# A recurrence feeding a gated MLP on one core: the hand-written start order, with the fourth group ahead of weight block 2

## The chip, the cores and the metric

One core of a Trainium2 chip runs the kernel. The metric is device time in microseconds (us): the median over runs of the time of the core. The kernel before takes 528.25 us, the median of 3 runs (527.22 to 528.74).

## The reference

```python
# attention part: B, H, S, D = 4, 8, 768, 48; state is D x D for each of the 32 (batch, head) pairs
for t in range(S):
    kt, vt, rt = k[:, :, t], v[:, :, t], r[:, :, t]
    cur = einsum('bhd,bhe->bhde', u * kt, vt)
    y[:, :, t] = einsum('bhd,bhde->bhe', rt, state + cur)
    state = w * state + einsum('bhd,bhe->bhde', kt, vt)
# MLP part: 3072 tokens, d_model 384, d_ff 1536
x = y.transpose(0, 2, 1, 3).reshape(B * S, H * D)
out = (sigmoid(x @ w_gate) * (x @ w_val)) @ w_out
```

## The kernel before

**Tiling.** The 768 time steps are cut into 12 chunks of 64 and the heads into 2 halves; a chunk and a half make a *group*, 24 in all, numbered in the order of work: group 0 and 1 are the halves of chunk 0, group 2 and 3 those of chunk 1, and so on. In a group the recurrence becomes small matmuls: scores of keys with queries, scores with values, queries with the state, and the outer products of keys and values that update the state. Two chunks together (512 tokens) are one tile of the MLP; the first tile is also worked in two parts of 256 tokens, the part of chunk 0 (`a`) and that of chunk 1 (`b`), so that the MLP can begin before chunk 1 is done. The MLP's 1536 inner columns are 12 blocks of 128, and a block of weights (gate, value and output together) is loaded once, joined from its 8-byte words and split into a rounded high part and a low rest; three matmuls make each product (lines 518 and 526 to 535). Block `0` in the start stands for what line 239 keeps in buffer 11.

**The order.** Tile's own scheduling is switched off (line 89): each engine runs its instructions in the order in which the program issues them. The first 60 to 70 us are written by hand: `START` (lines 43 to 58) is a list of steps, and the loop of lines 682 to 689 issues them one after the other. The rest follows from the loop of lines 711 to 743. An engine sees only its own steps of the list, so a step's place matters against the other steps of its engine.

The steps that are spoken of below, with `n` a group and `f` a weight block:

- `L.n`, `X.n`, `W.f` (SyncE): load the group's channels (queries and keys, line 104), its tokens (keys and values, line 109), a block's weights (line 242). Channels and tokens have 3 buffers each (lines 75 and 76), so `X.3` waits until the last reader of group 0's tokens, its outer products, is done.
- `F.n` (SyncE): six small transfers that bring x of one head pair into place in the MLP's input (line 501).
- `A.n`, `R.n` or `Rv.n`, `k.n`: keys with bonus (ScalarE, line 296), scaled queries (GpSimd or VectorE, line 309), scaled keys (VectorE, line 320). `T.n`, `Tv.n`: token keys (GpSimd, VectorE, line 324).
- `Z.n`, `K.n` (TensorE line 392, VectorE line 400): scores, and their copy out of PSUM under a mask.
- `I.n` (TensorE, line 354): the outputs of a group, queries with the state and then, behind a drain, scores with values. They go to two PSUM banks, called the group's pair here.
- `O.n` (TensorE, line 354): the outer products; for a group that `outer` names in line 426 they go to two accumulator banks, for others into the rest of the group's pair.
- `h.n` (ScalarE, line 493) and `l.n` (VectorE, line 497): x's high and low part out of the pair. `d.n` (ScalarE, line 447) and `s.n` (VectorE, line 466) or `sa.n` (ScalarE, line 468): the state decayed, and the outer products added or copied to it.
- `c.f`, `j.f`, `w.f`, `o.f` or `ov.f`: a weight block's upper halves taken out (ScalarE, line 249), words joined (VectorE, line 256), high part rounded (ScalarE, line 264), low rest (GpSimd or VectorE, line 267).
- `u.f`, `v.f` (TensorE, line 531): gate and value products of a block; `g.f` sigmoid (ScalarE, line 544), `m.f` product (VectorE, line 548), `H.f` high part (ScalarE, line 553), `q.f` or `qv.f` low part (line 557), `D.f` the output product (TensorE, line 573). A trailing `a` or `b` is a half of the first tile.
- `N.k` (TensorE, line 641): k matmuls of 128x512 on the identity, whose result nobody reads.

**PSUM.** A gate product, a value product and each half of a pair take one bank from a ring of three, in turn:

```python
    ring = ctx.enter_context(tc.tile_pool(name="ring", bufs=3, space=PSUM))   # line 72
        return ring.tile([P, 512], F32, name="ring")                          # line 84, one_bank
        yb[n] = one_bank(), one_bank()                                        # line 360, outputs
            w, o, k = (whi[f], wlo[f]), one_bank(), 0                         # line 527, up_one
```

So each new taker waits for the readers of what was taken three turns earlier. A pair's readers are `h`, `l` and `s` of its group; a gate product's reader is `g`, a value product's is `m`.

Of the kernel before, what the change touches and what calls it, by code (L numbers as in the profile page):

```python
# [40 lines left out]


START = """
ta L.0 tov.0 tc tb W.0 ts.0 L.1 ts.1 X.0 tz W.1 tk L.2 X.1 to.1 ti.1 X.2 ti.0 A.0 R.0 W.2 k.0 c0.0
tp tr Z.0 tt A.1 K.0 c0.1 tn k.1 I.0 Rv.1 j0.1 h.0 l.0 Tv.0 Z.1 c.1 j0.0 O.0 A.2 j.1 w0.0 sa.0 N.5
T.2 K.1 F.0 w.1 W.3 Rv.2 I.1 T.1 N.4 k.2 L.3 o0v.0 h.1 L.4 Z.2 w0.1 W.4 O.1 X.3 l.1 o0.1 s.1 u.0a
g.0a K.2 v.0a o.1 m.0a c.2 I.2 O.2 R.3 d.2 j.2 u.1a A.3 N.3 H.0a g.1a k.3 h.2 q.0a s.2 v.1a w.2 l.2
m.1a Z.3 T.3 A.4 H.1a N.4 R.4 K.3 c.3 k.4 I.3 O.3 F.2 L.5 W.8 o.2 D.0a X.4 h.3 L.6 Z.4 W.5 l.3 d.3
W.6 L.7 s.3 X.5 u.0b X.6 g.0b j.3 v.0b c.4 w.3 u.2 j.4 qv.1a m.0b H.0b g.2 v.2 q.0b K.4 w.4 Rv.5
u.1b T.4 A.5 v.1b g.1b m.1b D.0b k.5 H.1b I.4 ov.3 O.4 m.2 A.6 R.6 q.1b Z.5 k.6 L.8 d.4 D.1a W.7 h.4  # L50
o.4 s.4 H.2 D.1b K.5 c.6 l.4 Tv.5 u.3 c.5 g.3 j.6 v.3 j.5 qv.2 I.5 h.5 Z.6 l.5 R.7 L.9 A.7 m.3 X.8
d.5 D.2 ub K.6 H.3 O.5 k.7 s.5 w.5 q.3 u.4 c.8 T.6 ov.5 c.7 g.4 v.4 j.7 w.6 m.4 u.5 ov.6 g.5 v.5 I.6
Y.8 R.8 Z.7 W.9 d.6 O.6 W.10 X.7 w.7 W.11 H.4 s.6 X.9 D.3 j.8 h.6 qv.4 w.8 l.6 D.4 m.5 H.5 F.6 ov.7
qv.5 u.6 c.9 g.6 K.7 v.6 ov.8 m.6 Tv.7 H.6 u.7 qv.6 g.7 k.8 v.7 j.9 m.7 w.9 D.5 o.9 u.8 g.8 H.7 v.8
q.7 c.10 D.6 j.10 m.8 I.7 H.8 Z.8 O.7 d.7 R.9 h.7 w.10 s.7 D.7 b.8 ov.10 u.9 l.7 qv.8 g.9 c.11 v.9
F.7 Y.9 j.11 m.9 D.8 w.11 ov.11 u.10 g.10 H.9 qv.9 v.10 m.10 H.10 u.11 qv.10 g.11 t.8 i.8 v.11 K.8
k.9 m.11 D.9 H.11 t.9 D.10 q.11 b.9 T.9 i.9 T.8
"""


# [869 lines left out]
```

## Time and profile before

| | us |
|---|---|
| median of 3 runs | 528.25 (527.22 to 528.74) |
| the profiled execution's own time | 528.38 |
| its span, first to last instruction | 526.6 |
| TensorE busy | 509.7 (97% of the span) |
| VectorE, ScalarE, GpSimd busy | 202.6, 186.1, 187.2 (35 to 38%) |

The span is 1.78 us shorter than the execution's time. Busy shares are means over the whole span; the first 60 us differ from the rest, and that is where the change lies. In the rows of the timeline a row is a run of like instructions: its start in us from the start of the span, its length in us, engine, line, operation, and how many; a note in brackets is idle time of the engine ahead of it and what ended it. Matmul ends are modelled, so lengths between rows are taken from start to start.

### The profile page before, as it was taken

To read this page: it belongs to the slowest core of one execution; us is meant where nothing else is said; L and a number is where in the kernel's file an instruction comes from. 1 tells how busy PE (TensorE), PEld (TensorE's weight loads), DVE (VectorE), ACT (ScalarE), POOL (GpSimd) and SP (SyncE) were. 2 spreads that over 40 slices of the span, in tenths; PEclk is the share of its full clock that TensorE was granted. 3 is DMA by queue.
4 is the path that set the end of the run, shared out by engine and by line. 5 is a ranking of instruction groups with operands and counts; after the bars stand their busy time and mean duration, and the time that the engine had idled before them with its cause. 6 is when DMAs were issued, how large, how long until landed. Compare 5 with 4: busy or idle time off the path is not lost.

```text
span 526.6 us, 11976 instructions
## 1 busy us (share of the span) xinstructions
PE 509.7 (97%) x5220; PEld 421.4 (80%) x5220; DVE 202.6 (38%) x345; ACT 186.1 (35%) x395; POOL 187.2 (36%) x158
## 2 busy tenths in 40 slices
PE   3899999999999999999999999999999999999995
PEld 3689788888888788888888888888888888888884
DVE  7877865545242243242341432431442211111112
ACT  5587864534223134233133332331431221311211
POOL 4454402214545252453452452552352111111120
PEclk9899999999999999999999999999999999999999
DMA  8949654123213030420230420312400000100001
GB/s 318 368 144 421 262 191 167 34 75 96 76 64 88 10 107 4 145 88 19 78 98 12 148 87 1 97 36 72 147 17 2 11 7 14 61 0 1 0 2 65
DMA packets 15579, 47.84 MB, mean 91 GB/s; under 512 B 2368, under 2 KB 4928, under 8 KB 14112
## 3 DMA queue, kind: packets, MB, share of 16 engines
q1 hardware_dynamic: 15376, 46.74, 25.5%
q8 instruction: 43, 0.70, 0.6%
q10 hardware_dynamic: 144, 0.26, 0.1%
q14 instruction: 16, 0.13, 0.1%
HBM read 39.92 MB, written 4.72 MB: 85 GB/s over the span
## 4 chain that ended last, share of the span: by engine, by line
PE 95%; DVE 2%; DMA 1%; issue 1%; ACT 0%; SPq 0%; DVEq 0%; ACTq 0%
PE ring L531 56%; PE acc L573 29%; PE ring L354 7%; PE sc L392 3%; DMA chan<-in_ch 1%; DVE score L400 1%; DVE wf L256 0%; PE acc L641 0%; DVE chan L320 0%; ACT dec L296 0%; DVE sg L586 0%; DVE dec L309 0%; DVE xt L497 0%; DVE toks L324 0%; PE acc L354 0%
## 5 line engine op out<-in xcount | busy, mean ns | idle before, releaser
L531 PE MATMUL ring<-xt,wx 128*128 128x512 f32 (+1 forms) x1332 | 306.5, 384 | 0.0
L531 PEld LDWEIGHTS ring<-xt,wx 128*128 128x128 f32 x1332 | 245.2, 188 | 49.8 <-ACT sg L544 0.3
L557 POOL TENSOR_TENSOR h<-sg,h 128x512 fp32r<-128x512 f32 (+1 forms) x65 | 87.1, 1340 | 252.4 <-ACT h L553 252.4
L573 PE MATMUL acc<-h,wx 128*128 128x512 f32 (+1 forms) x666 | 161.3, 387 | 0.0
L573 PEld LDWEIGHTS acc<-h,wx 128*128 128x128 f32 x666 | 121.2, 188 | 25.0 <-DVE h L557 0.2
L548 DVE TENSOR_TENSOR sg<-ring,sg 128x512 f32<-128x512 f32 (+1 forms) x74 | 50.0, 676 | 235.0 <-PE ring L531 233.5
L544 ACT ACTIVATE sg<-ring 128x512 f32<-128x512 f32 (+1 forms) x74 | 43.2, 584 | 156.3 <-PE ring L531 156.3
L553 ACT CAST h<-sg 128x512 fp32r<-128x512 f32 (+1 forms) x74 | 45.0, 609 | 144.1 <-DVE sg L548 137.8
L309 POOL TENSOR_TENSOR dec<-chan,tabk 128x512 f32<-128x512 f32 x21 | 27.7, 1319 | 14.3 <-PE ring L354 14.0
L497 DVE TENSOR_TENSOR xt<-ring,xt 112x256 fp32r<-112x256 f32 (+1 forms) x52 | 19.9, 418 | 32.6 <-ACT xt L493 32.6
L324 POOL TENSOR_TENSOR toks<-toks,tabn 128x384 f32<-128x384 f32 x19 | 23.7, 1253 | 12.5 <-ACT wx L264 9.5
L330 POOL TENSOR_TENSOR dec<-dec,toks 128x384 f32<-128x384 f32 x16 | 16.3, 1017 | 26.9 <-DMA dec<-in_rt 26.7
L320 DVE TENSOR_TENSOR chan<-chan,tabk 128x512 f32<-128x512 f32 x24 | 24.8, 1034 | 0.6 <-ACT dec L296 0.6
L392 PE MATMUL sc<-dec,chan 48*64 48x64 f32 x768 | 17.2, 231 | 7.7 <-DVE chan L320 7.6
L400 DVE COPY_PREDICATED score<-masks,sc 128x512 f32<-128x512 int32 x32 | 23.9, 748 | 1.9 <-PE sc L392 1.1
L447 ACT ACTIVATE state<-state,pw 112x96 f32<-112x96 f32 x80 | 23.4, 362 | 1.8 <-PE ring L354 1.8
L392 PEld LDWEIGHTS sc<-dec,chan 48*64 48x64 f32 x768 | 14.8, 145 | 8.9 <-POOL dec L309 7.6
L466 DVE TENSOR_TENSOR state<-state,ring 48x192 f32<-48x192 f32 (+1 forms) x52 | 17.9, 350 | 8.1 <-PE ring L354 4.3
L256 DVE SCALAR_TENSOR_TENSOR wf<-wr,top 128x1152 int32<-128x1152 int32 (+1 forms) x13 | 16.8, 1304 | 9.5 <-ACT top L249 6.0
L354 PE MATMUL ring<-score,toks 64*48 64x64 f32 (+1 forms) x768 | 16.6, 223 | 3.7 <-issue 2.3
L493 ACT CAST xt<-ring 112x256 fp32r<-112x256 f32 (+1 forms) x52 | 16.7, 363 | 6.6 <-PE ring L354 6.4
L267 POOL TENSOR_TENSOR wx<-wf,wx 128x1152 fp32r<-128x1152 f32 (+1 forms) x5 | 12.5, 2507 | 18.3 <-ACT wx L264 18.3
(63 smaller groups left out, 254.7 us busy)
## 6 DMA issues: line engine op xcount, KB each, us to landing
wr<-in_wt SPq DMA_DIRECT2D x11, 1152.0 KB, 9.1
...
```

The costliest lines, as they stand in the source:

```text
L309: eng.tensor_tensor(v4(t[:, 0]), v4(chan[n][:, 0]), bc2(table_of(n)[:, :, ::-1]), ALU.mult)
L320: eng.tensor_tensor(v4(k), v4(k), bc2(table_of(n)), ALU.mult)
L324: eng.tensor_tensor(v4(k), v4(k), bc2(tabn[:, 4 * g : 4 * g + 4]), ALU.mult)
L354: nc.tensor.matmul(to[bank][64 * half : 64 * half + m, cs], lhsT, rhs, start=first, stop=stop, skip_group_check=True,)
L392: nc.tensor.matmul(sc[64 * gm : 64 * gm + 64, be, o : o + C], kk[row, cs : cs + C], rr[row, cs : cs + C], start=True, stop=True,)
L400: nc.vector.copy_predicated(t.rearrange("q (b m i) -> q b m i", b=2, m=4), masks[:, m].bitcast(I32).unsqueeze(1).unsqueeze(1).broadcast_to ...
L531: nc.tensor.matmul(o[:, self.cols], w[a][:, g * DM + kt * P : g * DM + (kt + 1) * P], self.x[:, kt, b, self.cols], start=(k == 0), stop=(k ...
L544: nc.scalar.activation(sg[:, c], self.pair[f][0][:, c], AF.Sigmoid, scale=UP)
L548: nc.vector.tensor_tensor(sg[:, c], self.pair.pop(f)[1][:, c], sg[:, c], ALU.mult)
L553: nc.scalar.copy(out=h[:, 0, c], in_=sg[:, c])
L557: eng.tensor_tensor(h[:, 1, c], self.sg.pop(f)[:, c], h[:, 0, c], ALU.subtract)
L573: nc.tensor.matmul(self.acc[d][:, self.cols], w[a][:, 2 * DM + d * P : 2 * DM + (d + 1) * P], h[:, b, self.cols], start=(f == 0 and k == 0 ...
```

## The change

In `START` the 188 steps between two unchanged ends become 185 in a new order. Group 3 comes earlier: `L.3` and `X.3` stand ahead of `W.2`, and `Z.3`, `K.3`, `I.3` and the work before them ahead of the preparing of block 2 (`j.2`, `w.2`) and of its products (`u.2`, `v.2`), which now come behind both halves of block 1. In chunk 0, group 0's outer products `O.0` go behind `I.1`, into accumulator banks, and their copy into the state (`sa.0`) goes behind group 1's copy of x (`h.1`). `W.3` and `W.4` are loaded behind `F.2`. Block 2's low rest moves from GpSimd to VectorE (`o.2` to `ov.2`), group 5's queries from VectorE to GpSimd (`Rv.5` to `R.5`). Of the 16 matmuls of `N` (`N.5`, `N.4`, `N.3`, `N.4`) one step of 7 is left. Nothing that is read later is left out.

```diff
-tp tr Z.0 tt A.1 K.0 c0.1 tn k.1 I.0 Rv.1 j0.1 h.0 l.0 Tv.0 Z.1 c.1 j0.0 O.0 A.2 j.1 w0.0 sa.0 N.5
-T.2 K.1 F.0 w.1 W.3 Rv.2 I.1 T.1 N.4 k.2 L.3 o0v.0 h.1 L.4 Z.2 w0.1 W.4 O.1 X.3 l.1 o0.1 s.1 u.0a
...
+Z.0 L.3 tt A.1 K.0 c0.1 tn k.1 I.0 Rv.1 j0.1 h.0 l.0 Tv.0 Z.1 c.1 j0.0 A.2 j.1 w0.0 T.1 N.7 w.1 T.2
+F.0 K.1 Rv.2 I.1 O.0 k.2 o0v.0 X.3 Z.2 L.4 R.3 h.1 W.2 w0.1 L.5 sa.0 l.1 O.1 o0.1 A.3 s.1 u.0a g.0a
...
     def outer(n):
         k, v = toks[n][:, 0], toks[n][:, 1]
-        if n in (1,):
+        if n in (0, 1):
             ob[n] = [pacc.tile([P, 512], F32, name=f"acc{i}") for i in (1, 2)]
```

**TensorE, between the first half of block 1's gate product and the outputs of group 3** (`u.1a` to `I.3`). Before, from the last idle matmul of `N.3` (`acc_540`) to the first of `N.4` (`acc_610`):

```order
L641 MATMUL acc_540<-spare 128x512
L531 MATMUL ring<-xt,wx 128x256 x9
L392 MATMUL sc<-dec,chan 64x64 x16
L392 MATMUL sc<-chan,dec 64x64 x16
L641 LDWEIGHTS spare
L641 MATMUL acc_610<-spare 128x512
```

and now, from `u.1a` to the first matmuls of `I.3`:

```order
L531 MATMUL ring<-xt,wx 128x256 x9
L392 MATMUL sc<-dec,chan 64x64 x16
L392 MATMUL sc<-chan,dec 64x64 x16
L531 MATMUL ring<-xt,wx 128x256 x9
L354 MATMUL ring<-dec,state 64x64 x2
```

The seven idle matmuls of this place are gone, and group 3's scores stand ahead of the value product `v.1a` instead of behind it.

**ScalarE, around the sigmoid of block 1's first half.** Line 249 with `wr_173` (before) and `wr_404` (now) takes out the upper halves of block 2's weights; the sigmoid of block 1's first half, `g.1a`, is the second row of line 544 of each order. Before:

```order
L544 ACTIVATE sg_450<-ring_440 128x256
L249 ACTIVATE top0_120<-wr_173 128x1152
L447 ACTIVATE state_99<-state_99,pw_101 112x96 x4
L296 ACTIVATE dec_518<-chan_365,wu_93 128x128 x4
L553 CAST h_544<-sg_450 128x256
L544 ACTIVATE sg_546<-ring_526 128x256
```

and now:

```order
L544 ACTIVATE sg_453<-ring_443 128x256
L447 ACTIVATE state_99<-state_99,pw_101 112x96 x4
L493 CAST xt_252<-ring_470 112x2x128
L493 CAST xt_252<-ring_471 112x2x128
L553 CAST h_537<-sg_453 128x256
L249 ACTIVATE top0_120<-wr_404 128x1152
L544 ACTIVATE sg_578<-ring_527 128x256
```

Now `g.1a` stands right behind line 249 instead of four rows after it, and the weights that line 249 reads are loaded later than before.

**VectorE, between the copy of group 5's x (`l.5`, line 497) and the adding to its state (`s.5`, line 466).** Before, with the joining of blocks 6 and 5 (line 256) ahead of `l.5`:

```order
L256 SCALAR_TENSOR_TENSOR wf_1001<-wr_742,top1_121 128x1152
L256 SCALAR_TENSOR_TENSOR wf_1013<-wr_732,top0_120 128x1152
L557 TENSOR_TENSOR h_971<-sg_795,h_971 128x512
L497 TENSOR_TENSOR xt_965<-ring_1016,xt_965 112x2x128
L497 TENSOR_TENSOR xt_965<-ring_1017,xt_965 112x2x128
L548 TENSOR_TENSOR sg_999<-ring_1003,sg_999 128x512
L400 COPY_PREDICATED score0_97<-masks_96,sc_1053 128x512 x2
L320 TENSOR_TENSOR chan_744<-chan_744,tabk_102 128x512
L466 TENSOR_TENSOR state_99<-state_99,ring_1016 112x2x96
```

and now:

```order
L497 TENSOR_TENSOR xt_874<-ring_1000,xt_874 112x2x128
L497 TENSOR_TENSOR xt_874<-ring_1001,xt_874 112x2x128
L256 SCALAR_TENSOR_TENSOR wf_1108<-wr_740,top1_121 128x1152
L256 SCALAR_TENSOR_TENSOR wf_1112<-wr_742,top0_120 128x1152
L400 COPY_PREDICATED score0_97<-masks_96,sc_1037 128x512 x2
L320 TENSOR_TENSOR chan_746<-chan_746,tabk_102 128x512
L466 TENSOR_TENSOR state_99<-state_99,ring_1000 112x2x96
```

The joining of blocks 6 and 5 now stands between `l.5` and `s.5`; on ScalarE the two instructions of line 249 that feed it (`c.6`, `c.5`) now stand behind `h.5` instead of well ahead of it.

## Rows read from the trace of the kernel before

**Rows 1.** Page, busy us of each engine, share of the span, instructions.
```profile
PE 509.7 (97%) x5220; PEld 421.4 (80%) x5220; DVE 202.6 (38%) x345; ACT 186.1 (35%) x395; POOL 187.2 (36%) x158
```

**Rows 2.** Windows: stretch, its length, busy us per engine, granted clock, DMA share, GB/s.
```profile
18.00:20.00 2.00, 0.63 (x25) 0.41 (x15) 2.00 (x3) 0.00 (x0) 1.00 (x1) 0.97 0.80 180
20.00:22.00 2.00, 2.00 (x12) 0.62 (x16) 1.38 (x4) 1.90 (x5) 0.00 (x0) 0.50 0.86 343
22.00:24.00 2.00, 2.00 (x97) 1.95 (x93) 0.52 (x2) 0.24 (x1) 1.69 (x2) 0.68 0.98 387
```

**Rows 3.** Timeline of TensorE, from `O.0` to `u.0a`.
```profile
14.26 1.09 PE L354 MATMUL ring<-toks 64*64 64x48 f32 x32
15.29 1.81 PE L641 MATMUL acc<-spare 128*128 128x512 bf16 x5
17.63 0.56 PE L354 MATMUL ring<-score,toks 64*64 64x64 f32 x20 [0.53 <-DVE score L400]
19.56 0.43 PE L354 MATMUL ring<-score,toks 64*48 64x64 f32 x12 [1.37 <-issue]
19.92 1.89 PE L641 MATMUL acc<-spare 128*128 128x512 bf16 x4
21.74 1.14 PE L392 MATMUL sc<-dec,chan 48*64 48x64 f32 x32
...
23.41 0.62 PE L354 MATMUL acc<-toks 64*64 64x48 f32 x32
23.96 2.51 PE L531 MATMUL ring<-xt,wx 128*128 128x256 f32 x18
```

**Rows 4.** Timeline of TensorE, from `N.3` to `I.3`.
```profile
29.61 0.82 PE L641 MATMUL acc<-spare 128*128 128x512 bf16 x3
30.24 1.35 PE L531 MATMUL ring<-xt,wx 128*128 128x256 f32 x9
...
32.61 1.04 PE L641 MATMUL acc<-spare 128*128 128x512 bf16 x4
33.58 0.68 PE L354 MATMUL ring<-dec,state 48*64 48x64 f32 x32
```

**Rows 5.** Page's DMA issues: a block's weights, KB each, median us from issue to landing.
```profile
wr<-in_wt SPq DMA_DIRECT2D x11, 1152.0 KB, 9.1
```

**Rows 6.** Timeline of ScalarE: `g.1a`, then `c.6` with `c.5`, then `h.5`.
```profile
29.81 0.38 ACT L544 ACTIVATE sg<-ring 128x256 f32<-128x256 f32 x1 [0.21 <-PE ring L531]
...
52.98 2.90 ACT L249 ACTIVATE top<-wr 128x1152 f16<-128x1152 bf16 x2 [0.41 <-DMA wr<-in_wt]
...
58.61 0.65 ACT L493 CAST xt<-ring 112x256 fp32r<-112x256 f32 x2 [2.30 <-PE ring L354]
```

**Rows 7.** Timeline of TensorE: `Z.6` (first of two rows), `D.2`, `O.5`, `u.4` and on.
```profile
58.35 0.65 PE L392 MATMUL sc<-dec,chan 48*64 48x64 f32 x32
...
59.40 2.33 PE L573 MATMUL acc<-h,wx 128*128 128x512 f32 x9
61.66 0.67 PE L354 MATMUL ring<-toks 64*64 64x48 f32 x32
62.26 8.48 PE L531 MATMUL ring<-xt,wx 128*128 128x512 f32 x36
```

**Rows 8.** Timeline of VectorE: `k.5`, `ov.3`, `j.6` with `j.5`, `K.6`, `k.7`, `s.5`.
```profile
47.19 0.68 DVE L320 TENSOR_TENSOR chan<-chan,tabk 128x512 f32<-128x512 f32 x1
47.79 1.35 DVE L267 TENSOR_TENSOR wx<-wf,wx 128x1152 fp32r<-128x1152 f32 x1
...
55.66 2.62 DVE L256 SCALAR_TENSOR_TENSOR wf<-wr,top 128x1152 int32<-128x1152 int32 x2
...
61.15 1.52 DVE L400 COPY_PREDICATED score<-masks,sc 128x512 f32<-128x512 int32 x2
62.56 1.43 DVE L320 TENSOR_TENSOR chan<-chan,tabk 128x512 f32<-128x512 f32 x1
63.92 0.61 DVE L466 TENSOR_TENSOR state<-state,ring 112x192 f32<-112x192 f32 x2
```

More of the change, by code (lines that the diff above doesn't have):

```diff
@@ L43 @@
 START = """
-ta L.0 tov.0 tc tb W.0 ts.0 L.1 ts.1 X.0 tz W.1 tk L.2 X.1 to.1 ti.1 X.2 ti.0 A.0 R.0 W.2 k.0 c0.0
-tp tr Z.0 tt A.1 K.0 c0.1 tn k.1 I.0 Rv.1 j0.1 h.0 l.0 Tv.0 Z.1 c.1 j0.0 O.0 A.2 j.1 w0.0 sa.0 N.5
-T.2 K.1 F.0 w.1 W.3 Rv.2 I.1 T.1 N.4 k.2 L.3 o0v.0 h.1 L.4 Z.2 w0.1 W.4 O.1 X.3 l.1 o0.1 s.1 u.0a
-g.0a K.2 v.0a o.1 m.0a c.2 I.2 O.2 R.3 d.2 j.2 u.1a A.3 N.3 H.0a g.1a k.3 h.2 q.0a s.2 v.1a w.2 l.2
-m.1a Z.3 T.3 A.4 H.1a N.4 R.4 K.3 c.3 k.4 I.3 O.3 F.2 L.5 W.8 o.2 D.0a X.4 h.3 L.6 Z.4 W.5 l.3 d.3
@@ L49 @@
[L49 to L57, printed above, removed]
+ta L.0 tov.0 tc tb W.0 ts.0 L.1 ts.1 X.0 tz W.1 tk L.2 X.1 to.1 ti.1 X.2 ti.0 A.0 R.0 k.0 c0.0 tp tr
+Z.0 L.3 tt A.1 K.0 c0.1 tn k.1 I.0 Rv.1 j0.1 h.0 l.0 Tv.0 Z.1 c.1 j0.0 A.2 j.1 w0.0 T.1 N.7 w.1 T.2
@@ new lines @@
+F.0 K.1 Rv.2 I.1 O.0 k.2 o0v.0 X.3 Z.2 L.4 R.3 h.1 W.2 w0.1 L.5 sa.0 l.1 O.1 o0.1 A.3 s.1 u.0a g.0a
+K.2 v.0a o.1 m.0a k.3 I.2 O.2 d.2 h.2 u.1a H.0a s.2 l.2 q.0a Z.3 c.2 g.1a T.3 v.1a K.3 A.4 m.1a R.4
+H.1a I.3 k.4 qv.1a D.0a F.2 R.5 X.4 h.3 Z.4 W.3 W.4 l.3 d.3 X.5 D.1a L.6 A.5 O.3 W.6 W.5 s.3 L.7
+u.0b X.6 g.0b j.2 v.0b m.0b H.0b u.1b W.8 q.0b K.4 w.2 v.1b g.1b k.5 m.1b T.4 D.0b H.1b q.1b I.4 c.3
+ov.2 O.4 h.4 l.4 d.4 u.2 R.6 s.4 g.2 j.3 v.2 w.3 m.2 Z.5 H.2 L.8 ov.3 D.1b W.7 c.4 K.5 A.6 qv.2 u.3
@@ new lines @@
+g.3 j.4 k.6 v.3 Tv.5 w.4 m.3 I.5 h.5 Z.6 l.5 o.4 L.9 X.8 c.6 R.7 D.2 ub c.5 O.5 j.6 H.3 j.5 A.7 q.3
+u.4 d.5 T.6 K.6 w.5 k.7 s.5 c.8 ov.5 c.7 g.4 v.4 j.7 w.6 m.4 ov.6 u.5 g.5 v.5 I.6 Y.8 R.8 Z.7 W.9
+d.6 O.6 W.10 X.7 w.7 W.11 H.4 s.6 X.9 D.3 j.8 h.6 qv.4 w.8 l.6 D.4 m.5 H.5 F.6 ov.7 qv.5 u.6 c.9 g.6
+K.7 v.6 ov.8 m.6 Tv.7 H.6 u.7 qv.6 g.7 k.8 v.7 j.9 m.7 w.9 D.5 o.9 u.8 g.8 H.7 v.8 q.7 c.10 D.6 j.10
+m.8 I.7 H.8 Z.8 O.7 d.7 R.9 h.7 w.10 s.7 D.7 b.8 ov.10 u.9 l.7 qv.8 g.9 c.11 v.9 F.7 Y.9 j.11 m.9
@@ L58 @@
+D.8 w.11 ov.11 u.10 g.10 H.9 qv.9 v.10 m.10 H.10 u.11 qv.10 g.11 t.8 i.8 v.11 K.8 k.9 m.11 D.9 H.11
+t.9 D.10 q.11 b.9 T.9 i.9 T.8
 """
```

## The prediction, made before the changed kernel ran

> **What bounds the kernel now.** I read the page first, for the busy shares, then the windows of the first 60 us, then the timeline of TensorE there, and last the timelines of the engines that it waits for. The page says that TensorE is busy for 509.7 of 526.6 us [rows 1], so a change of order can only win what TensorE loses by waiting, by running slowly, or by work that nobody needs. All three lie early. The reader is to see four things. First, 16 matmuls of line 641 produce nothing: groups of 5, 4, 3 and 4 [rows 3, 4]. Second, the outputs of group 1 break off after 20 of 32 records and go on 1.37 us later, with no engine named as the cause (row at 19.56, "issue") [rows 3]. Third, the granted clock: TensorE is busy for 0.63 of the 2 us from 18 on, and in the next 2 us the grant is 0.50, so 1.2 GHz; over 22 to 24 it is 0.68 on average, so full, 2.4 GHz, returned near 23.3 [rows 2]. Fourth, from `u.0a` on (23.96) TensorE hardly stops, so time saved early moves all that follows, unless a new wait takes it back.
>
> **The change, part by part.** I follow TensorE from 14.26 on and count gains against before as negative.
>
> *Idle matmuls up to 17.6.* `N.5` becomes `N.7` and begins at 14.26, where `O.0` was. Seven at 0.36 us (1.81 for 5) end near 16.8, and at 0.47 (1.89 for 4) near 17.5. The next work, `I.1`, starts at 17.63 because it waits for the score copy on VectorE [rows 3], whose own queue up to there is as before. So this costs and wins nothing: that wait covers it.
>
> *`O.0` behind `I.1`, `N.4` gone.* I leave the break in place up to 19.56, since nothing in the trace ties it to a particular wait; it falls into `I.1` or into `O.0`. Behind it stood the rest of `I.1` (0.36, 19.56 to 19.92) and `N.4` (1.82, to 21.74) [rows 3]. Now the rest of `O.0` stands there: between nothing and its whole 1.03 us (14.26 to 15.29); I take 0.45, as about half the records stood behind the break before. `Z.2` then starts at 20.0 instead of 21.74. But it runs wholly at 1.2 GHz: 1.8 us, against 1.67 (21.74 to 23.41), to 21.8. `O.1` takes 1.0 at that clock, like `O.0`, against 0.55 (23.41 to 23.96). So `u.0a` starts at 22.8, and loses 0.25 while the clock is still low. Gain: **0.9**. Bounds: 0, if the weights of block 0 and the state copy `sa.0`, now behind `h.1` on ScalarE, hold `u.0a` as long as before; 1.7, if none of the 1.8 us is given back to the clock.
>
> *`N.3` and the second `N.4` gone.* Start to start they took 0.63 (29.61 to 30.24) and 0.97 (32.61 to 33.58) [rows 4]. The second filled the time in which VectorE copied group 3's scores; now `v.1a`, nine matmuls that took 1.3 us, stands between `Z.3` and `I.3` and covers that copy. Gain: **1.6**; I give it no bounds beyond those of the waits that follow.
>
> *Block 2's load late: a new wait for group 3.* `W.2` now stands behind `X.3` and `L.4` on SyncE, and `X.3` waits for the end of `O.0` at 20.0; so do `L.5` and `F.2` behind them. With two loads ahead I estimate its issue at 21; the median of such a load is 9.1 us to landing [rows 5], so it lands near 30.1. ScalarE meets `c.2` (1.45, half of 2.90) directly ahead of the sigmoid `g.1a` (0.38) [rows 6]: done near 31.9. The second bank of group 3's pair is the one that `u.1a` took three turns earlier, so `I.3` waits for `g.1a`. Without that it would start at 33.58 less 2.5, at 31.1. Loss: 0.8 with the median load, 0 if the load lands 2 us sooner; I take **0.5**, nearer to the row.
>
> *Block 2 and 3 on VectorE.* `ov.3` now follows `m.2` directly, some 2.0 us (0.68 and 1.35) [rows 8] behind the end of `v.2`; TensorE meanwhile has a score step (1.05, 58.35 to 59.40) and a half `D` (half of 2.26, 59.40 to 61.66) [rows 7], 2.2 us. I cost it at nothing, with 0.3 as the upper bound. `W.3` and `W.4` behind `F.2` are hidden by blocks 0 and 1, whose second halves now come first.
>
> *`c.6`, `c.5`, `j.6`, `j.5` between `h.5` and `s.5`: a new wait for block 4.* In the ring of three banks `v.4` takes the one whose last reader is the first instruction of `s.5`. Count from the end of `I.5`, where `Z.6` starts (58.35) [rows 7]. Before, `u.4` started 3.9 us later (62.26) and its nine matmuls took 2.1 (a quarter of 8.48): `v.4` could start at 6.0, and `s.5`'s first half was done at 5.9 (63.92 and 0.3) [rows 8], just in time. Now ScalarE has `h.5` (from 0.26 to 0.8; a row runs some 0.1 over its successor's start, as 61.15 and 1.52 against 62.56 show), then `c.6` and `c.5` (2.90) to 3.7 [rows 6]; VectorE has `j.5` behind `c.5` (1.31, half of 2.62) to 5.0, `K.6` (1.41, 61.15 to 62.56) to 6.4, `k.7`, and half of `s.5`. `k.7` took 1.43 where it stands, its like `k.5` 0.68 [rows 8]. So the bank comes free at 7.4 to 8.15: TensorE waits 1.4 to 2.15 us. Loss: **1.7**, near the middle.
>
> That upper end has a rule beside it. The Trainium skill, "SBUF — State Buffer", section "Who interferes with whom", says that a VectorE instruction with two inputs in SBUF and a GpSimd instruction that reads SBUF shut each other out for a whole instruction. By that rule `k.7`, which stands beside token keys on GpSimd, would keep its 1.43 and the sum would be about 0.4 us worse.
>
> *The sum.* 0.9 and 1.6 gained, 0.5 and 1.7 lost: **0.3 us faster**. Best ends: 1.7 and 1.6 gained, 1.4 lost, 1.9 faster. Worst: 1.6 gained, 0.8, 0.3 and 2.15 lost, 1.65 slower. The profiled execution took 528.38; this makes 528.1. The median of the runs is 0.13 lower, so I forecast **527.95 us**; own range 526.35 to 529.9. A measurement of this kernel can tell about 0.3% from no change, 1.6 us: the likeliest case is no change.
>
> **The rivals.**
>
> *The break shrinks and the clock does not fall (faster).* Less is in flight at 17 to 19 us, as `L.3` (512 KB) and not `W.2` (1152 KB) is loaded then; if the break of 1.37 us is a matter of that traffic, it shortens, and the stretch at 1.2 GHz (19.9 to 23.3, so 1.7 us of its 3.4 lost) may not come. Of 3.1 us I take half, since block 0's weights then hold `u.0a`: 526.4. Against it: no row names traffic as the cause.
>
> *The wait for block 4 does not form (faster).* If ScalarE and VectorE run ahead there, the 1.7 goes: 526.25. For it: both have idle time on the page (35 and 38% busy) [rows 1]. Against it: each link of the chain hangs on `h.5`, and so on the end of `I.5`, in a fixed order.
>
> *The clock stays low (slower).* Nine idle matmuls are gone, four of them from the very stretch in which the grant is 0.50. If full clock returns one such stretch later, 1.7 more is lost: 529.65, and 530.1 with the upper end of the wait for block 4. It decides at about 24 us: if the grant is still 0.50 beyond that, this is the case. Against it: scores and outer products keep TensorE busy in that stretch, and the grant rose at 23.3 after a stretch half of which was scores and outer products [rows 2, 3].
>
> The Trainium skill, "TensorE: Matmul & The Clock Gate", section "Why this matters for your kernels", asks to keep TensorE busy without long gaps, since an idle engine is set back to half rate. By that rule the removal of idle matmuls speaks against this change. The trace agrees that the grant fell behind a stretch with little work (0.63 of 2 us); that it would stay low with real work in place of idle matmuls no row shows.
>
> **How the numbers follow.** Likeliest case 0.55, mostly within 1.6 us, 0.05 of it faster and 0.02 slower. Shrunken break 0.17, of which 0.13 beyond the bound; no wait for block 4 0.13, of which 0.10; low clock 0.15, of which 0.08 slower by over 0.3%. So faster 0.28, slower 0.10, same 0.62. The range for 8 in 10, 526.2 to 529.8, takes in the likeliest case nearly whole and the centres of all three rivals.
>
> **What would show it.** In the changed kernel's profile: no rows of line 641 behind 17.6 us; `u.0a` near 22.8; `I.3` near 31.6 with a wait of half a microsecond for ScalarE's line 544; `I.5` some 2 us earlier than 57.0; then one idle time of 1.4 to 2.1 us ahead of `v.4`, released by VectorE's line 466, with lines 256 and 400 just ahead of it. From there on every step should stand within 1 us of before. I am wrong if that wait is missing, if the break at 18 to 19.6 has another length, or if the grant falls a second time.

## The result, and the profile after

The changed kernel took **531.46 us** (median of 8 runs, 529.06 to 532.72), before beside it 528.50 (8 runs, 527.22 to 529.06): ratio 1.0055, 95% interval 1.0033 to 1.0077. The forecast was 527.95 with a range of 526.2 to 529.8 and no change as the likeliest case; the kernel is slower.

The profiled execution of the changed kernel took 529.06, with a span of 527.3. It is the fastest of its eight; the others have spans of 528.0 to 530.9 and mean granted clocks down to 0.992, against 0.997 in the profile. So there are two questions: why the best execution is 0.7 us longer than the one shown of before, and why the rest scatter above it. Scatter is not the changed kernel's alone: in the experiments 35 executions of before, side by side with the changed kernel, lie between 526.65 and 532.68.

Page of the changed kernel, busy us of each engine (before: [rows 1]), and its row on the instruction queue (packets, MB, share of 16 engines):

```profile
PE 507.7 (96%) x5211; PEld 420.0 (80%) x5211; DVE 203.9 (39%) x345; ACT 186.8 (35%) x395; POOL 185.9 (35%) x158
...
q8 instruction: 43, 0.70, 0.6%
```

Windows of the changed kernel over the stretch of [rows 2]:

```profile
18.00:20.00 2.00, 1.61 (x108) 1.48 (x101) 2.00 (x4) 1.53 (x5) 0.94 (x1) 1.00 0.10 24
20.00:22.00 2.00, 1.28 (x60) 1.12 (x52) 1.43 (x5) 1.98 (x7) 2.00 (x2) 1.00 0.77 223
22.00:24.00 2.00, 2.00 (x18) 2.00 (x18) 1.95 (x4) 0.73 (x3) 2.00 (x2) 1.00 1.08 408
```

TensorE is 2 us less busy, and the clock stays full where before had a stretch at half rate. Timeline of TensorE in the changed kernel, `I.1` to `u.0a` (before: [rows 3]), then group 3's scores, `v.1a` and `I.3` (before: [rows 4]), then `D.1a`, the step behind it and `D.1b`, then `I.5` to `I.6` (before: [rows 7]):

```profile
17.64 0.68 PE L354 MATMUL ring<-score,toks 64*64 64x64 f32 x32 [0.86 <-DVE score L400]
18.14 0.51 PE L354 MATMUL acc<-toks 64*48 64x48 f32 x18
19.04 0.38 PE L354 MATMUL acc<-toks 64*64 64x48 f32 x13 [0.39 <-issue]
...
21.10 0.79 PE L354 MATMUL acc<-toks 64*64 64x48 f32 x32 [0.71 <-ACT state L468]
21.82 2.42 PE L531 MATMUL ring<-xt,wx 128*128 128x256 f32 x18
...
27.47 0.56 PE L392 MATMUL sc<-dec,chan 48*64 48x64 f32 x19
28.40 0.39 PE L392 MATMUL sc<-dec,chan 48*64 48x64 f32 x11 [0.38 <-issue]
...
29.25 1.33 PE L531 MATMUL ring<-xt,wx 128*128 128x256 f32 x9
30.51 0.68 PE L354 MATMUL ring<-dec,state 48*64 48x64 f32 x32
31.46 0.68 PE L354 MATMUL ring<-score,toks 64*64 64x64 f32 x32 [0.26 <-DVE sg L548]
...
34.42 1.34 PE L573 MATMUL acc<-h,wx 128*128 128x256 f32 x9
35.69 0.67 PE L354 MATMUL ring<-toks 64*64 64x48 f32 x32
...
49.40 1.33 PE L573 MATMUL acc<-h,wx 128*128 128x256 f32 x9
...
55.18 0.68 PE L354 MATMUL ring<-dec,state 48*64 48x64 f32 x32
...
59.93 0.43 PE L354 MATMUL ring<-toks 64*64 64x48 f32 x13
60.53 0.47 PE L354 MATMUL ring<-toks 64*48 64x48 f32 x19 [0.17 <-issue]
60.93 2.33 PE L531 MATMUL ring<-xt,wx 128*128 128x512 f32 x9
64.77 6.42 PE L531 MATMUL ring<-xt,wx 128*128 128x512 f32 x27 [1.51 <-DVE state L466]
71.12 0.68 PE L354 MATMUL ring<-dec,state 48*64 48x64 f32 x32
```

The kernel before at `Z.3` (its first row), `D.1a` with `D.1b`, `I.5` and `I.6`:

```profile
31.52 0.69 PE L392 MATMUL sc<-dec,chan 48*64 48x64 f32 x32
...
50.56 2.42 PE L573 MATMUL acc<-h,wx 128*128 128x256 f32 x18
...
57.02 0.68 PE L354 MATMUL ring<-dec,state 48*64 48x64 f32 x32
...
70.68 0.68 PE L354 MATMUL ring<-dec,state 48*64 48x64 f32 x32
```

| start of | before | changed | difference |
|---|---|---|---|
| `u.0a` | 23.96 | 21.82 | -2.14 |
| `I.5` | 57.02 | 55.18 | -1.84 |
| `I.6` | 70.68 | 71.12 | +0.44 |
| end of the span | 526.6 | 527.3 | +0.7 |

At each of these places the same real work is done in both. The change wins 2.14 us up to `u.0a`. From there to `I.5` it loses 0.3 although 7 idle matmuls (1.6 us) are gone. From `I.5` to `I.6` it loses 2.3: the new wait ahead of `v.4` is a row of 1.51 and makes `u.4` to `v.5` 1.77 longer from start to start (60.93 to 71.12, before 62.26 to 70.68), and `O.5`, broken off after 13 matmuls, takes 1.00 instead of 0.60. Timeline of VectorE in the changed kernel on the way to `s.5` (before: [rows 8]):

```profile
57.28 0.76 DVE L497 TENSOR_TENSOR xt<-ring,xt 112x256 fp32r<-112x256 f32 x2 [1.23 <-ACT xt L493]
59.00 2.78 DVE L256 SCALAR_TENSOR_TENSOR wf<-wr,top 128x1152 int32<-128x1152 int32 x2 [0.96 <-ACT top L249]
61.70 1.54 DVE L400 COPY_PREDICATED score<-masks,sc 128x512 f32<-128x512 int32 x2
63.14 1.31 DVE L320 TENSOR_TENSOR chan<-chan,tabk 128x512 f32<-128x512 f32 x1
64.38 0.61 DVE L466 TENSOR_TENSOR state<-state,ring 112x192 f32<-112x192 f32 x2
```

### The profile page after: what moved, and what is told of

Its sections match the earlier page's. It is cut to its first block, busy times and chain, and to the rows that moved or that the text cites. A ratio compares the mean times of both kernels' runs of the same rounds, so it can differ in the third digit from the quotient of the medians.

```text
span 527.3 us, 11961 instructions
## 1 busy us (share of the span) xinstructions
PE 507.7 (96%) x5211; PEld 420.0 (80%) x5211; DVE 203.9 (39%) x345; ACT 186.8 (35%) x395; POOL 185.9 (35%) x158
## 4 chain that ended last, share of the span: by engine, by line
PE 87%; DVE 0%; issue 0%; DVEq 0%
PE ring L531 52%; PE acc L573 27%; PE ring L354 5%; PE sc L392 2%; DVE sg L586 0%; PE ring L221 0%; DVEq L586 0%; DVE state L466 0%
## 5 line engine op out<-in xcount | busy, mean ns | idle before, releaser
L309 POOL TENSOR_TENSOR dec<-chan,tabk 128x512 f32<-128x512 f32 x22 | 29.2, 1328 | 14.0 <-issue 8.1
L249 ACT ACTIVATE top<-wr 128x1152 f16<-128x1152 bf16 (+1 forms) x13 | 18.2, 1423 | 1.1 <-DMA wr<-in_wt 1.1
```

Of the source, the lines that this page charges most:

```text
L309: eng.tensor_tensor(v4(t[:, 0]), v4(chan[n][:, 0]), bc2(table_of(n)[:, :, ::-1]), ALU.mult)
```

## The experiments

Three suspects were open: the wait ahead of `v.4`, the missing idle matmuls, and the breaks that the timeline calls "issue". Each ratio is to before on the same chip, over all executions of both, so it can differ from the ratio of the medians. The kernels e1 to e8 and e13 to e16 ran on one chip, e9 to e12 on a second, e17 and e18 on a third; the median of before beside them was 529.53 (e1 to e4), 529.16 (e5 to e8), 529.34 (e13 to e16), 529.14 and 529.46. Of e16 and e18 there is one execution each, profiled.

| kernel | median us (runs) | ratio to before, 95% |
|---|---|---|
| changed (e1) | 530.08 (12) | 1.0021, 1.0000 to 1.0042 |
| idle matmuls back (e2) | 532.24 (12) | 1.0045, 1.0020 to 1.0071 |
| `s.5` early (e3) | 529.55 (12) | 1.0002, 0.9981 to 1.0024 |
| before, less idle matmuls (e4) | 529.60 (12) | 1.0009, 0.9989 to 1.0030 |
| `W.2` late (e5) | 532.78 (9) | 1.0077, 1.0049 to 1.0105 |
| `s.5`, `ov.5` early (e6) | 529.47 (12) | 1.0021, 1.0002 to 1.0039 |
| e5 and e6 (e7) | 531.05 (12) | 1.0036, 1.0020 to 1.0053 |
| e6 and `N.3` back (e8) | 529.06 (12) | 1.0001, 0.9986 to 1.0016 |
| e8, `sa.0` and `g.4` early (e9) | 529.03 (12) | 0.9993, 0.9976 to 1.0010 |
| e9, `K.1` early (e10) | 530.64 (12) | 1.0026, 1.0008 to 1.0043 |
| changed, counts shifted (e11) | 532.90 (7) | 1.0065, 1.0046 to 1.0084 |
| e9, counts shifted (e12) | 530.45 (12) | 1.0031, 1.0015 to 1.0048 |
| e9, `R.3` late (e13) | 528.65 (12) | 0.9994, 0.9974 to 1.0015 |
| e13, `W.2` early (e14) | 530.96 (12) | 1.0029, 1.0012 to 1.0047 |
| changed (e15) | 531.40 (12) | 1.0039, 1.0018 to 1.0060 |
| e13 with `N.6` (e17) | 528.77 (12) | 1.0002, 0.9982 to 1.0022 |

### The changed kernel again, three times

> The changed kernel once more, for the spread of its executions and a second profile. Clock theory (the removed idle matmuls let the granted clock rise late or fall again in the first 35 us in most executions): the executions spread over 527 to 531 us of span, the long ones with a mean granted clock near 0.992 and the short ones near 0.997 or more; a profile of a long one shows 2 to 4 us more at 0.50 ahead of 35 us, and the same waits otherwise. Wait theory (the new idle time ahead of block 4's value product, 1.51 us in the first profile, is all there is): every execution about 1 us above before, so 529.5, and no link with the clock.

> The changed kernel, on the same chip as the two others of this list. If its loss against before is its own and not the first chip's: 0.2 to 0.6% over before again, wait ahead of v.4 1.4 to 2.0 us, breaks behind 450, 962 or 2242 TensorE instructions of 0.1 to 2.5 us together, and both kernels above 1 us or more under it. If the first result was the chip's: within 0.1% of before.

> The changed kernel once more, for one more profile. If the spread of its executions comes from the loading of instructions and the clock: span above or below 528.0 us by as much as the breaks behind 450, 962 and 2242 instructions and half the length of a stretch at granted clock 0.50 tell, within 0.5 us; the wait ahead of v.4 differs by under 0.3 us from 1.6. If by the wait ahead of v.4: that wait differs as the span does.

In two later comparisons it was slower again, the first time by an interval that begins at 1.0000. The three profiles have spans of 528.2, 534.8 and 528.4 us. The wait ahead of `v.4` is in all of them and hardly differs: 1.75, 1.86, 1.76. What differs is the break in the first half of group 3's scores, always behind 19 matmuls of `Z.3`: 0.68, 2.20 and 0.83 us (0.38 above), and, in the long execution, the clock. In the other two it is full up to 524 us; they are 0.9 and 1.1 us longer than the first through a longer break, 0.25 more at `v.4`, up to 0.4 behind the last matmul and, in e1, 0.5 at `u.0a`, of which 0.3 to 0.5 is won back at `O.5` and `u.3`. Timeline of TensorE in the long execution (e15):

```profile
27.55 0.56 PE L392 MATMUL sc<-dec,chan 48*64 48x64 f32 x19
30.31 0.59 PE L392 MATMUL sc<-dec,chan 48*64 48x64 f32 x11 [2.20 <-issue]
...
70.39 8.05 PE L531 MATMUL ring<-xt,wx 128*128 128x512 f32 x27 [1.86 <-DVE state L466]
```

Windows of the same execution:

```profile
28.00:32.00 4.00, 1.80 (x52) 1.57 (x47) 0.23 (x2) 2.25 (x6) 2.39 (x3) 0.74 0.16 37
32.00:36.00 4.00, 3.74 (x65) 3.35 (x69) 2.73 (x5) 0.41 (x1) 0.70 (x1) 0.50 0.56 158
36.00:40.00 4.00, 4.00 (x79) 3.66 (x75) 1.69 (x4) 3.35 (x11) 0.67 (x1) 0.50 0.99 413
40.00:44.00 4.00, 4.00 (x79) 3.75 (x76) 1.51 (x3) 0.75 (x3) 0.00 (x0) 0.98 1.02 416
...
70.00:76.00 6.00, 5.61 (x18) 4.48 (x19) 4.92 (x7) 3.92 (x4) 0.00 (x0) 0.72 0.00 0
```

At each of the two idle times the grant falls to half rate: from 29.9, still within the break, to 40.2, and from 70.9, behind the wait, to 74.3. Comparing the starts of the same matmuls in the first profile and in this one tells what each part costs: 1.8 us for the longer break, 4.1 over the first stretch at half rate (to 40.3), 0.35 for the longer wait and 1.6 over the second stretch; 0.7 is won back between them, as there is no break in `O.5` and no wait ahead of `u.3` here. With 0.4 in small pieces that makes the 7.5 by which this span is the longer one. The wait ahead of `v.4` explains 0.35 of it; in this execution the scatter comes from the break and from the clock.

### Are the idle matmuls what is missing?

The idle matmuls were put back where before had them (e2), and taken out of the kernel before (e4; `N.5` stays):

```diff
-I.1 O.0 k.2
+I.1 O.0 N.4 k.2
...
-u.1a H.0a
+u.1a N.3 H.0a
...
-Z.3 c.2
+Z.3 N.4 c.2
```

and in e4, from the list of before:

```diff
-T.1 N.4 k.2
+T.1 k.2
...
-A.3 N.3 H.0a
+A.3 H.0a
...
-H.1a N.4 R.4
+H.1a R.4
```

> The changed kernel with the removed idle matmuls put back: 4 behind the outer products of group 0, 3 behind the first half of block 1's gate product, 4 behind the scores of group 3. Clock theory: the median falls by about 2 us, to 529.5, the spread narrows to that of before, and the mean granted clock is 0.995 or more in nearly all executions, although TensorE does up to 2.4 us of useless work. Wait theory: the time stays or grows by up to 2.4 us, to 531.5 to 534.

> The kernel before without its idle matmuls behind the first five (N.4, N.3 and N.4 left out, nothing else changed). Clock theory: slower by 1 to 3 us, to 529.5 to 531.5, with mean granted clocks near 0.992 in many executions. Rival (idle matmuls only take time that TensorE could work in): faster by 1 to 2 us, 527 us, with the clocks of before.

Both theories get half. With the matmuls back no break stood in the profile at all, but the kernel was not faster (1.0045, against 1.0021 for the changed kernel beside it, with intervals that overlap): the matmuls take their time, the wait ahead of `v.4` (1.91) stayed, and the clock fell behind it (0.50 over 68 to 70 us). Without them before was not faster either, at a ratio of 1.0009: idle times took their place (0.47, 0.41, 0.70, 0.65, 0.94 and 1.14 us between 18 and 34 us; before had the one of 1.37 and others of up to 0.29), the grant fell behind the last of them, and its runs show clocks down to 0.988. So the 11 removed idle matmuls, 3.4 us in the rows of before (1.82, 0.63 and 0.97), win nothing measurable in the old order, and this cannot be read from their rows.

### Taking the wait ahead of `v.4` away

The state of group 5 is added right after the joining of block 5, ahead of `K.6`; in e6 `ov.5` goes ahead of `K.6` too, and e8 is e6 with `N.3` behind `u.1a`. Edit of e6:

```diff
-c.5 O.5 j.6 H.3 j.5 A.7 q.3 u.4 d.5 T.6 K.6 w.5 k.7 s.5 c.8 ov.5 c.7 g.4
+c.5 O.5 j.6 d.5 j.5 s.5 w.5 H.3 A.7 q.3 u.4 T.6 ov.5 K.6 k.7 c.8 c.7 g.4
```

> The changed kernel with group 5's state update ahead of the score copy and the scaled keys on VectorE (its decay ahead of the high part of block 3 on ScalarE, block 5's low rest ahead of the scaled keys), so that the bank of block 4's value product comes free about 2 us sooner. Wait theory: the 1.5 us of idle time ahead of that product goes, and the median falls by 1.2 to 1.5 us, to 530.1; the spread stays. Clock theory alone: the spread and the clocks stay as in the changed kernel, and the median falls only by what that idle time cost, so the two add. Rival: the wait moves to block 5's low rest and the time stays at 531.5.

> The changed kernel with d.5, j.5 and s.5 right behind j.6 (the joining of block 5 and the adding to the state ahead of the score copy K.6), and ov.5 ahead of K.6, since ov.5 was late by 0.49 us for u.5 when only s.5 was moved. If the wait ahead of v.4 is all that takes the change's gain: that wait under 0.3 us, none over 0.3 ahead of u.5, span 526.0 to 526.6 (527.3 to 528.2 less 1.5), time 1.0 to 1.7 us under the changed kernel and faster than before by 0.5 to 1.2. If the breaks of TensorE's instruction supply and the clock falls behind them decide: the wait goes but the time is within 0.5 us of the changed kernel, with a break of over 1 us or granted clock 0.50 somewhere between 18 and 45 us.

> The kernel with s.5 and ov.5 early, and the three idle matmuls N.3 put back behind u.1a (0.63 us of work in three instructions). If idle matmuls ahead of the group's scores only cost their time: 0.6 us over the kernel with s.5 and ov.5 early. If they hide the loading of instructions and keep the clock up: no break over 0.2 us in the scores of group 3, no clock fall from 24 to 45 us, and a time equal to or under that kernel's, by 0 to 1 us.

In all three profiles the wait is gone (e3 has 0.49 ahead of `u.5` for `ov.5` in its place, e8 0.50 ahead of `v.5` for `g.4`). The times are 1.0002, 1.0021 and 1.0001 of before; on this chip only e8's interval lies below one of the changed kernel's (e15's). The profile of e3 has the break in `Z.3` at 2.28 us, and a grant of 0.50 over 32 to 40 us behind it. What took the gain in e6, its timeline of TensorE shows, in `O.5`:

```profile
60.24 0.44 PE L354 MATMUL ring<-toks 64*64 64x48 f32 x13
61.85 0.47 PE L354 MATMUL ring<-toks 64*48 64x48 f32 x19 [1.17 <-issue]
```

The break of 0.17 behind 13 matmuls of `O.5` has become 1.17: of the 1.5 us that the wait gave back, the break took 1.0. In e8 it stood behind 10 of them (0.29). Three idle matmuls more ahead, three matmuls of the step less: the first sign that breaks are tied to counts.

### What the breaks are

Count all TensorE instructions of the trace, weight loads, drains and waits too. Then the breaks of before (in `I.1`), of the changed kernel (in `O.0`, `Z.3`, `O.5`) and of the kernels above stand at number 450, 706, 962 or 2242: at 450, and multiples of 256 from there. (The "issue" times of 0.15 to 0.29 us inside `I.n` are another thing: they stand behind its drain, at any count.) To test it, the seven matmuls of `N.7` were cut into four of 128 columns each, in the changed kernel (e11) and in e9 (e12): the same columns, 42 instructions more ahead of 17.6 us.

```diff
-                t.rearrange("q (a n) -> q a n", a=2), bits[:, 0:P],
-                bits.unsqueeze(1).broadcast_to([P, 2, 2 * P]), start=True, stop=True,
+            for q in range(4) if k == 7 else ():
+                nc.tensor.matmul(t[:, 0:P], bits[:, 0:P], bits[:, 0:P], start=True, stop=True)
```

> The changed kernel with each of the seven idle matmuls of N.7 cut into four of 128 columns: the same columns, 21 matmuls and their weight loads more, so 42 TensorE instructions more ahead of 17.6 us. If the breaks of TensorE stand behind fixed counts of its instructions (450, 962 and 2242 in the profile, 256 apart or a multiple of it): each moves 21 matmuls towards the start of the program, from behind 18 matmuls of O.0 to behind 29 of I.1, from behind 19 of the second half of Z.3's to behind 7 of the 9 of u.1a, and from behind 13 of O.5 to behind the first of D.2, where it may be hidden. If a break belongs to a step (its data, its semaphores): it stays in O.0, Z.3 and O.5. Time: that of the changed kernel within 1 us by either.

> The first kernel of this list with the seven idle matmuls cut into four each, as above, which moves the counts by 42 instructions. If the counts matter, the breaks that are left in it (0.3 us in O.5) move into D.2, whose matmuls are long, and the time is 0 to 0.5 us under that of the first kernel; if they don't, equal within 0.3 us.

Timeline of TensorE in e11, in `u.1a`:

```profile
26.19 1.10 PE L531 MATMUL ring<-xt,wx 128*128 128x256 f32 x7
28.06 0.40 PE L531 MATMUL ring<-xt,wx 128*128 128x256 f32 x2 [0.77 <-issue]
```

Timeline of TensorE in e12, in `I.1`:

```profile
17.65 0.68 PE L354 MATMUL ring<-score,toks 64*64 64x64 f32 x29 [0.69 <-DVE score L400]
19.18 0.26 PE L354 MATMUL ring<-score,toks 64*48 64x64 f32 x2 [0.85 <-issue]
```

Behind 7 of the 9 matmuls of `u.1a` in e11, and behind 29 of `I.1` in e12, as expected (the 19 matmuls of `Z.3` in the expectation are of its first half). The break in `O.5` is gone too, but that shows little: three of the changed kernel's four profiles have none there either. A wait for data would have stayed with its step. The cause is TensorE's own instructions: the queue of kind "instruction" moves them in packets of 16 KB (0.70 MB in 43, page above), and in 20 profiles each of the 30 such breaks of over 0.1 us ends 2.24 to 2.67 us after the start of such a packet. The Trainium skill, "Runtime: NRT & Kernel Launch", section "Instruction fetch mechanics", says that an engine's instructions are refilled in blocks of 16 KiB, 256 of them, over a DMA queue of its own; the counts and the packets agree. It calls the cost of a boundary mostly hidden; here up to 2.3 us of it shows.

What a shift is worth was not forecast so well: e12 was slower than e9 on the same chip (1.0031 against 0.9993), and e11 at 1.0065 is above the changed kernel's 1.0055, 1.0021 and 1.0039, though its interval meets the first and the last of these and the changed kernel did not run on this chip. One boundary leaves `O.5`, the others fall badly: e12 has breaks of 0.85, 0.60 and 0.70.

### What holds the packets up

In e15 the 706th instruction was reached at 23.83 us, and the packet for the 962nd started at 27.80. Queues in the DMA view of e15, from 23.85 to 27.70 and then from 27.70 to 28.00 (packets, MB, share of 16 engines):

```profile
q1 hardware_dynamic: 239, 1.28, 80.6%
...
q8 instruction: 1, 0.02, 20.6%
```

For 4 us bulk loads keep the DMA engines 81% busy and no instruction packet moves; it moves when they thin out. In the 20 profiles the packet for instruction 962 starts between 0.1 us ahead of the start of instruction 706 and 4.3 us behind it. The load in flight there is block 2, which the change moved to about 20 us (issued at 19.7 in e15). So `W.2` was moved again: behind `F.2` (e5, with `c.2` behind `A.5`; e7 is e5 with e6), or directly behind `F.0`, near 18.8 us (e14, on top of e13).

```diff
-h.1 W.2 w0.1
+h.1 w0.1
...
-F.2 R.5
+F.2 W.2 R.5
...
-Z.3 c.2 g.1a
+Z.3 g.1a
...
-A.5 O.3
+A.5 c.2 O.3
```

and in e14:

```diff
-F.0 K.1
+F.0 W.2 K.1
...
-sa.0 W.2 w0.1
+sa.0 w0.1
```

> The changed kernel with block 2's weights W.2 loaded behind F.2, and their upper halves c.2 taken out behind A.5, so that 1152 KB less are in flight from 20 to 29 us. If the break behind TensorE's first outer products (0.38 us in the first profile of the changed kernel, 0.68 in the second, 2.28 with s.5 early) is loading of instructions that bulk weights hold up: under 0.3 us here, no clock fall behind it, the wait of 1.5 to 1.8 us ahead of v.4 as before, time 0.3 to 0.8 us under the changed kernel. If the break does not hang on the traffic: 0.4 us or more again, time equal to the changed kernel within 0.3 us.

> Both edits together, W.2 and c.2 late and s.5 and ov.5 early. If both the wait ahead of v.4 and the break behind group 3's scores take the gain, and the break is a matter of traffic: the shortest of these four, 1.5 to 2.3 us under the changed kernel. If the break does not hang on traffic: equal to the kernel with s.5 and ov.5 early within 0.3 us.

> The same, and W.2 directly behind F.0 on SyncE, near 18.2 instead of 20 to 21 us. If the packet of the instruction queue that group 3's scores wait for is held up by the load of block 2 (it started 1.0 us behind the 706th TensorE instruction with W.2 late, 1.8 to 4.2 us behind it with W.2 at 20 to 21): it starts within 1.8 us, the break behind instruction 962 is under 0.2 us, and the time is 0.3 to 1.2 us under the kernel without this edit, 0.5 to 1.5 under before. If the traffic moves the trouble one step ahead: a break at the 706th instruction or in O.0 longer by 0.5 us or more, time equal within 0.3 us.

> The kernel with W.2 early once more, for one more profile: its first profile had no break (span 526.5) but 9 of its 12 executions a clock of 0.991 to 0.994 and 2 to 4 us more. If the load ahead of group 1's outputs holds up the packet for the first break, or the tokens: a break behind 450 instructions or a wait ahead of I.1 or Z.2 of over 0.8 us, and the granted clock at 0.50 from about 20 us on. If not there: the fall stands behind a later wait, and the profile shows where.

Late, the packet for 962 came 1.0 us behind the 706th instruction in e5 and 0.1 ahead of it in e7, and neither has a break there. That fits the theory of the traffic, in one profile each; the time expected from it did not come. In e7 the break in `O.5` is 1.46. In e5 `c.2` now waits 3.29 us for the load, and on ScalarE `g.0b` stands behind it, whose bank `v.1b` takes. Timeline of TensorE in e5, `v.1b` and then `D.0b`:

```profile
41.02 1.34 PE L531 MATMUL ring<-xt,wx 128*128 128x256 f32 x9 [1.56 <-ACT sg L544]
42.83 2.29 PE L573 MATMUL acc<-h,wx 128*128 128x256 f32 x9 [0.47 <-ACT h L553]
```

Early, the first profile had no break (span 526.5), and the packet for 706 started 0.8 us behind the 450th instruction. Yet the median was 530.96, and the second profile (e18, span 528.9) shows why. Its timeline of TensorE, in the products of block 0:

```profile
21.14 2.28 PE L531 MATMUL ring<-xt,wx 128*128 128x256 f32 x16
25.75 0.50 PE L531 MATMUL ring<-xt,wx 128*128 128x256 f32 x2 [2.33 <-issue]
```

Its windows behind that:

```profile
27.00:29.00 2.00, 1.85 (x66) 1.79 (x67) 0.40 (x2) 1.33 (x6) 0.00 (x0) 0.73 0.11 39
29.00:31.00 2.00, 2.00 (x11) 1.63 (x10) 1.28 (x4) 2.00 (x4) 1.39 (x2) 0.50 0.06 12
```

Here the packet for 706 started 4.2 us behind the 450th instruction, with `W.2` in flight. The load takes its break along: at 20 us it meets the packet for 962, at 18.8 us, in one of two profiles, the one for 706.

### The other waits

From e8 on three more edits: `sa.0` right behind `h.1` and `g.4` ahead of `c.8` (e9); on top of it `K.1` ahead of `j.1` and `w.1` behind `w0.1` (e10), or `R.3` behind `o.1` (e13), and that with `N.6` for `N.3` (e17).

```diff
-h.1 W.2 w0.1 L.5 sa.0 l.1
+h.1 sa.0 W.2 w0.1 L.5 l.1
...
-k.7 c.8 c.7 g.4
+k.7 c.7 g.4 c.8
```

in e10:

```diff
-A.2 j.1 w0.0
+A.2 K.1 j.1 w0.0
```

and in e13:

```diff
-L.4 R.3 h.1
+L.4 h.1
...
-o.1 m.0a
+o.1 R.3 m.0a
```

> The kernel with s.5 and ov.5 early and N.3 back, and in addition sa.0 right behind h.1 on ScalarE (ahead of w0.1), and g.4 ahead of c.8. There O.1 waited 1.05 us for sa.0 and v.5 0.50 us for g.4. If these waits were on the path that sets the end: under 0.5 us ahead of O.1, none ahead of v.5, and a time 0.8 to 1.2 us under that kernel's, so 0.5 to 1.2 us under before. If the loading of TensorE's instructions takes it back: the waits go, a break behind the same count of TensorE instructions (0.3 us or more, a packet of the instruction queue some 2.4 us ahead of its end) is longer by as much, and the time is equal to that kernel's within 0.4 us.

> The same with group 1's score copy K.1 ahead of j.1 on VectorE and w.1 behind w0.1 on ScalarE, so that I.1 starts 0.6 us earlier, when T.1 is done on GpSimd near 17.0. If waits alone decide: 0.6 us under the kernel before it in this list. If instruction loading paces TensorE here: I.1 earlier by 0.6, but the first break (within O.0, 18 matmuls into it) longer by 0.3 to 0.6, and the time equal within 0.3 us.

> The kernel with s.5, ov.5, sa.0 and g.4 early and N.3 back, and in addition R.3 (GpSimd) behind o.1 instead of ahead of h.1. There u.0a waited 0.98 us for l.1, whose forerunner o0v.0 took 1.85 us beside R.3 (0.75 in the first profile of the changed kernel). If that collision is the cause: o0v.0 near 0.75, the wait ahead of u.0a under 0.3, and a time 0.5 to 1.0 us under the kernel without this edit. If T.2 on GpSimd lengthens VectorE's work as well: o0v.0 or the instruction ahead of it still above 1 us in the profile, gain under 0.4. If instruction loading takes it back: the break in group 3's scores (1.21 us in that kernel's profile) is as long or longer, and the time equal within 0.3.

> The kernel with R.3 late, and N.6 instead of N.3 behind u.1a: 0.6 us more of idle matmuls in six more TensorE instructions ahead of group 3's scores. There a break of 1.30 us stood behind 962 instructions, and 4 of 12 executions were 2 us or more above the rest at a clock of 0.994. If the matmuls turn a break into work and so keep the clock up: break under 0.8 us, no granted clock of 0.50 between 20 and 75 us, no such slow executions, median 0.2 to 1.0 us under before. If they only cost their time: 0.4 to 0.6 us over the kernel with R.3 late.

In e9 both waits (that of `O.1` for `sa.0`, that of `v.5` for `g.4`) go, and the time stays: `u.0a` now waits 0.98 us for `l.1` on VectorE, and the break in `Z.3` is 1.21. In e10 `I.1` starts 1.2 us earlier and the break in `O.0` grows to 1.38, so that its second part begins at 18.80 where e9 has 18.95; VectorE then runs beside GpSimd, and `Z.2` waits 1.53 more. In e13 the collision is gone. VectorE's `o0v.0` in e9, beside `R.3` on GpSimd:

```profile
19.06 1.85 DVE L267 TENSOR_TENSOR wx<-wf,wx 128x576 fp32r<-128x576 f32 x1
```

and in e13, with GpSimd idle:

```profile
19.03 0.74 DVE L267 TENSOR_TENSOR wx<-wf,wx 128x576 fp32r<-128x576 f32 x1
```

The Trainium skill, "SBUF — State Buffer", section "Who interferes with whom", has the two shut each other out, and this pair agrees. The wait ahead of `u.0a` goes, `u.0a` starts at 21.10 and the span is 526.4, but the break in `Z.3` is 1.30 and 4 of 12 runs are above 530. In e17 six idle matmuls move that break to behind 12 matmuls of `Z.3` and cut it to 0.18, with one of 0.42 at instruction 706 that e13 does not have, and 2 of 12 runs are above 530; the ratio, 1.0002, is no lower. None of the 14 other versions beats before. The lowest ratios, e9's 0.9993 and e13's 0.9994 (0.9974 to 1.0015), are as fast as before; e13 is faster than the changed kernel on the same chip (e15, 1.0039, 1.0018 to 1.0060).

## Why the prediction was wrong

- **Idle matmuls up to 17.6: nothing, as taken.** `I.1` starts at 17.64, before at 17.63.
- **`O.0` behind `I.1`: 0.9 forecast, with 1.7 as the upper bound, 2.14 measured.** The order was right. What failed is that the break would keep its length and the grant fall: the break was 0.39 us instead of 1.37, and the clock stayed full. That is the first rival (chance 0.17), in whose favour the thinner traffic at 17 to 19 us was named. How much of the shorter break is traffic is not shown: the packet for instruction 450 started only 0.19 us earlier (16.70, before 16.89), and with the whole of `I.1` ahead of it that instruction was due later. A row of the page could have pointed at the cause, that of the instruction queue; it was not read. The length of the break did not set `u.0a` either: the other three profiles of the changed kernel have none in `O.0`, and `O.1` starts at 21.1 to 21.2 in all four, after 0.70 to 0.82 us of waiting for `sa.0` on ScalarE, which the sum had only as a bound.
- **"`N.3` and the second `N.4` gone. ... Gain: 1.6; I give it no bounds beyond those of the waits that follow."** This is the step that failed. From `u.0a` to `I.5` the time went from 33.06 to 33.36 us, where 1.1 less was forecast. The 1.60 is gone, and 1.90 came in its place, start to start: 0.69 in `Z.3`, which holds the break (1.78, before 1.09); 0.59 where `D.1a` and `D.1b`, before in one piece with `u.3` and `v.3` (6.46), now stand apart (1.27 and 5.78, with a wait of 0.14 ahead of `u.3`); and 0.62 in pieces of at most 0.21, among them the gate and value products, split by steps of groups. That splitting costs this is read from the rows and was not tried by itself. Why the break came is shown: idle matmuls are long work in few instructions. With them TensorE took 5.9 us from its 706th to its 962nd instruction, and the packet, 3.4 us behind the 706th, came just in time; in the changed kernel it came after 2.3, but TensorE was through with its work after 4.3 and waited 0.38, in other executions 0.7 to 2.2.
- **`W.2` late, 0.5 lost: did not form.** The load landed at 28.15, where 30.1 was estimated. ScalarE waited 0.86 us for it, but `g.1a` (29.54, 0.37 us) was done while TensorE was still at `v.1a` (to 30.51), and `I.3` started at 30.51 without a wait for line 544; the forecast was 31.6. The load costs something else: it holds up the packet.
- **`ov.3` ahead of `u.3`: nothing forecast, 0.3 as the bound, 0.14 measured** as idle time ahead of `u.3`. (The 0.68 that the prediction takes for `m.2` is the row of `k.5`.)
- **The new wait ahead of `v.4`: 1.7 forecast, 1.51 measured** (1.77 start to start) and 1.75 to 1.91 in other profiles, released by line 466, with lines 256, 400 and 320 ahead of it as forecast; `k.7` took 1.31, near the upper of the two values. `I.5` was 1.84 earlier where 2 was forecast. This step was right, but taking the wait away does not give its whole length back: in e6 the break in `O.5`, just ahead, grew by 1.0.
- **The clock.** The third rival had the clock stay low beyond 24 us and named the missing idle matmuls. In the profile it never falls ahead of 524 us; in e15 it falls twice, at the break and behind the `v.4` wait. It was the right danger, at the wrong place and without the cause of the idle time.
- **The range.** It was made against one execution. Before varied by 1.84 us over its eight runs, the changed kernel by 3.66, and before by 6.03 over the 35 runs beside e1. The profiles of the changed kernel show breaks and falls that differ from run to run, and the sum has no term for them. The sum with the profiled execution (0.3 faster forecast, 0.7 slower measured) was off by 1.0, the median by 3.5. That the first was so near is partly luck: 1.2 more gained at `u.0a` and 0.5 not lost for `W.2` set off most of what failed behind them.

What stays open: few of the longer executions are profiled (e3, e15 and e18 above all) and only one of before, so that how often each break or fall occurs in either kernel is not shown, nor how the 3.5 us of the median divide among them. The changed kernel's loss was 0.55% in the first comparison and 0.21 and 0.39% in the later two; why these differ was not tried.
